# Gating logits accumulated in one bank, turned by one transposition in layer 1's banks, and one expert's weights loaded from ScalarE's queue

## Chip, core and metric

One NeuronCore of a Trainium2 chip runs the whole program as one launch. The metric is device time in microseconds (us), the median of repeated executions. TensorE does the products, VectorE, ScalarE and GpSimd the work around them, and SyncE issues most transfers. In the profile these are PE (PEld is its weight load), DVE, ACT, POOL and SP. PSUM, the memory into which TensorE writes, has eight banks of 128 partitions by 512 fp32 values.

## What is computed

A chunked attention feeds a feed-forward layer, and that feeds a mixture of experts with two experts per token:

```python
scores = scale * np.matmul(q_c, k_c.transpose(0, 1, 2, 4, 3))     # chunks of 64, 8 heads of 64
attn = softmax(scores); x = np.matmul(attn, v_c)                  # 4608 tokens of 512
h = x @ w_in; x = (h - np.tanh(h)) @ w_out                        # 512 -> 2048 -> 512
noisy_logits = x @ w_gate + np.log1p(np.exp(x @ w_noise)) * noise # 8 experts
top2 = np.argpartition(-noisy_logits, 2, axis=1)[:, :2]           # with softmax weights over the two
out[mask] += top2_w[mask, k, None] * (np.maximum(x[mask] @ w1[e], 0.0) @ w2[e])
```

## The kernel before

**Tiles and steps.** The 4608 tokens are 36 tiles of 128, in nine groups of four (g = 0 to 8). The first part of the program runs each group through the feed-forward layer in 16 steps. A step is one block of 128 of the 2048 hidden units: twelve layer-1 products (`products1`, L338; fp32 as a high and a low fp32r part, three passes over four blocks of 128) into a bank named `hp`, then `activate` (ScalarE's tanh L374, VectorE's subtraction L377 that is the last to read the bank, ScalarE's L378 and VectorE's L380 that make the two parts), and twelve layer-2 products (`products2`, L446) of the step before into four banks named `acc`. There are two `hp` banks, taken in turn by whoever asks next. The second part runs 24 groups of slots (three for each of 8 experts) in 8 steps each; there the activation is L382 on ScalarE and L385 on VectorE.

**Half-steps.** `advance` emits a step: layer 1 and its activation, the functions listed for slot h, layer 2 of the step before, the functions of slot h + 1. So an even slot stands between layer 1 and layer 2 and an odd slot behind layer 2. A group has 32 slots (`H1`), a slot group 16 (`H2`). The lists are written out by hand: `hs` for attention visits, a second `hs` for the gating of the group before, and loops for loads. Each engine runs its own instructions in the order emitted and waits for the others' semaphores.

**What stands in the slots.** An attention visit (`u_attn`) transposes the exponentials of one tile (`u_t`, L198, into an `hp` bank named `pt` that ScalarE copies out at L200), multiplies those of an older tile with v and makes the scores of a new tile (`products`, L144, in the two banks named `pair`); it then loads q, k and v of the tile two visits later on SyncE's queue. `load_v` waits until the visit's products have read the old buffer, and what is behind it on that queue waits too. The gating of group g - 1 runs within group g: `u_z` and `u_yt` load the layer's output back and transpose it in blocks of 32 on VectorE (`x2t`, L499); `u_lg` (L523) multiplies each tile's four blocks with the gate weights `wg` into the four quarters of the partitions, 512 columns in all, which ScalarE copies to `ls` (L526); `u_gate` (L542) sums the quarters and turns them with four small products against `summat`, a matrix made by `sums`. Then come short VectorE operations (`u_gate2` to `u_gate2m`), GpSimd's `u_gate3` with the running count of each expert, and `u_pos` (L640, L641), two products that give each token its place. All of these take a bank of `pair` by `misc`. Behind `u_pos` the rows are reloaded (`yr`) and scattered by GpSimd.

**Loads of experts.** `fetch_e` loads one block of an expert's two weight matrices on SyncE's queue (L282, two buffers for each of the two), and `prep_e` splits it three slots later into two parts: ScalarE L321, then VectorE or GpSimd L323. Expert 0 is loaded in group 8, expert 1 in the first two slot groups. In the second slot group `dispatched` waits until the scattered rows have landed and then issues the first loads of gathered rows (`xg`, L503) on the same queue.

The last group's gating (group 8) runs in the first slot group. The lists that set these places:

```python
hs = (1, 5, 11, 15, 20, 26) if g == 1 else (5, 14, 20, 26)              # visits
hs = (9, 11, 12, 13, 17, 18, 19, 19, 20, 23)                            # u_lg, u_gate, ..., u_gate3, u_pos
hs = (9, 12, 14, 16, 18, 19, 21, 21, 23, 24)                            # the same for g == 1
```

Of the kernel before, what the change touches and what calls it, by code (L numbers as in the profile page):

```python
# [9 lines left out]
F32 = mybir.dt.float32  # L10
# [5 lines left out]
ALU = mybir.AluOpType  # L16
# [15 lines left out]
def moe_chain_kernel(ctx: ExitStack, tc: tile.TileContext, q, k, v, w_in, w_out, wgn, noise,  # L32
                     w1, w2, out):
    nc = tc.nc
# [3 lines left out]
    NG = len(GS)  # L38
    G0 = [sum(GS[:g]) for g in range(NG)]
# [43 lines left out]
    def bank():  # L83
        return pools["pair"][:, after("pair", 2)]

    def misc(*shape):
        n = 1
        for m in shape:
            n *= m
        p = bank()[:, :n]  # L90
        return p.rearrange("p (a b) -> p a b", b=shape[1]) if len(shape) > 1 else p

    place = {G0[g] + j: (g, j) for g in range(NG) for j in range(GS[g])}
# [182 lines left out]
        nc.vector.tensor_tensor(xt[:, 1, :, c0:c0 + n], ps[:, :, :n], hi.bitcast(F32),  # L276
                                op=ALU.subtract)

    def fetch(src, tag, f=None):
        if src.dtype == F32:  # L280
            x = blk("st", "q" if tag == "wa" else "e", 2)
            nc.sync.dma_start(x, src)  # L282
            return x
        x = raws[tag][f].rearrange("p s m -> p (s m)")
        nc.sync.dma_start(x, src.bitcast(U32))
        return x
# [229 lines left out]

    def u_lg(g):
        n = GS[g]
        p = misc(n, 128)
        for j in range(n):  # L520
            x = X2T.pop(G0[g] + j)
            for d in range(4):
                nc.tensor.matmul(p[32 * d:32 * d + 32, j, :], lhsT=wg[:, d, :], rhs=x[:, d, :],  # L523
                                 start=True, stop=True, tile_position=(0, 32 * d))
        LS[g] = sp.tile([128, 4, 128], F32, name="ls", bufs=1)[:, :n]
        nc.scalar.copy(LS[g], p)  # L526

    def small(name, shape, dt=F32, bufs=1):
# [8 lines left out]

    def u_gate(g):
        n, i0 = GS[g], G0[g]
        p = misc(n, 16)  # L540
        for j in range(n):
            nc.tensor.matmul(p[:, j, :], lhsT=LS[g][:, j], rhs=summat, start=True, stop=True)  # L542
        lg = small("lg", [128, 4, 16])[:, :n, :]
        nc.scalar.copy(lg, p)
        t = small("t", [128, 4, 8])[:, :n, :]
        z = lg[:, :, 8:16]
        nc.vector.scalar_tensor_tensor(t, z, -1.0, z, op0=ALU.mult, op1=ALU.min)
        nc.scalar.activation(t, t, AF.Exp)
        GT[g] = lg, t, NZ.pop(g)
# [86 lines left out]
    def u_pos(g):  # L636
        n = GS[g]
        pay, ef, oh, mk = GT.pop(g)
        p = misc(n, 8)
        nc.tensor.matmul(p, lhsT=lower, rhs=mk[:, 0], start=True, stop=False)  # L640
        nc.tensor.matmul(p, lhsT=ones, rhs=mk[:, 1], start=False, stop=True)  # L641
        ve = nc.vector
        ps = small("ps_", [128, 4, 8])[:, :n, :]
        if g >= NG - 2:
            ve.tensor_tensor(ps, p, bump[:, None, :].to_broadcast([128, n, 8]), op=ALU.add)
        else:
            ve.tensor_copy(ps, p)
        for kk in range(2):
            ve.tensor_tensor(oh[:, :, kk, :], oh[:, :, kk, :], ps, op=ALU.mult)
        pk = small("pk", [128, 8, 1])[:, :2 * n]  # L650
        ve.reduce_sum(pk, oh.rearrange("p g k e -> p (g k) e"), axis=AX.X)
        sh = small("sh", [128, 8, 1])[:, :2 * n]
        ve.tensor_scalar(sh, pk, float(CAP), float(SHIFT), op0=ALU.is_ge, op1=ALU.mult)
        pi = small("pi", [128, 8], I32)[:, :2 * n]
        ve.tensor_tensor(pi, pk[:, :, 0], sh[:, :, 0], op=ALU.add)
        efk = ef.rearrange("p g k -> p (g k)")
        lo = small("lo_", [128, 8], I32)[:, :2 * n]
        ve.tensor_scalar(lo, pi, 127, None, op0=ALU.bitwise_and)
        hi = small("hi_", [128, 8], I32)[:, :2 * n]
        ve.tensor_scalar(hi, pi, 7, None, op0=ALU.arith_shift_right)  # L660
        fl = small("fl", [128, 8])[:, :2 * n]
        ve.scalar_tensor_tensor(fl, lo, float(NCOL), hi, op0=ALU.mult, op1=ALU.add)
        row = sp.tile([128, 2, 8], I32, name="row", bufs=2)[:, :, :2 * n]
        ve.scalar_tensor_tensor(row[:, 0], efk, float(LROWS), pi, op0=ALU.mult, op1=ALU.add)
        ve.scalar_tensor_tensor(row[:, 1], efk, float(LROWS), fl, op0=ALU.mult, op1=ALU.add)

        def scatter(to, at, src, group):
            s = nc.gpsimd.indirect_dma_start(  # L668
                out=to, out_offset=bass.IndirectOffsetOnAxis(ap=at, axis=0),
                in_=src, in_offset=None)  # L670
            tc.declare_no_dep(s.ins, group=group, reason="distinct rows")
            tc.add_to_no_dep_group(group, s.ins)
            if to is xs and g >= NG - 2:
                tc.declare_no_dep(s.ins, group="sealed", reason="bump: no rows below SEAL")
                tc.add_to_no_dep_group("late", s.ins)

        def reload(j):
            i = G0[g] + j
            y = blk("yr", "y", 4)
            nc.sync.dma_start(y, x2d[i * 128:(i + 1) * 128, :])  # L680

            def both():
                for kk in range(2):
                    c = 2 * j + kk
                    nc.gpsimd.memset(spacer, 0.0)
                    scatter(xs, row[:, 0, c:c + 1], y, "rows")
                rows_left.pop()
            loaded.append(both)

        for j in range(n):  # L690
            rows_left.append(j)
            waiting.append(L(reload, j))
        for j in range(n):
            for kk in range(2):
                c = 2 * j + kk
                waiting.append(L(scatter, lst, row[:, 1, c:c + 1], pay[:, j, kk, :], "entries"))
# [136 lines left out]
    ident = cp.tile([128, 128], F32, name="ident")  # L833
    make_identity(nc, ident)
    wg = cp.tile([128, 4, 32], F32, name="wg")
    summat = cp.tile([128, 16], F32, name="summat")
    lower = cp.tile([128, 128], BF16, name="lower")
    ones = cp.tile([128, 128], BF16, name="ones")
    nc.vector.memset(ones, 1.0)
# [8 lines left out]
    def consts():  # L848
# [12 lines left out]
        nc.vector.memset(pad, 0)  # L861
        nc.gpsimd.iota(pad[:, :, 0], pattern=[[0, NCOL // 4], [128, 4]], base=0,
                       channel_multiplier=1)

    def sums():
        nc.vector.tensor_tensor(summat, ident[:, 0:16], ident[:, 32:48], op=ALU.add)
        nc.vector.tensor_tensor(summat, summat, ident[:, 64:80], op=ALU.add)
        nc.vector.tensor_tensor(summat, summat, ident[:, 96:112], op=ALU.add)

    def store_consts():  # L870
        nc.sync.dma_start(wg[:, :, 0:16], wgn.rearrange("p (d m) -> p d m", d=4))
# [73 lines left out]
    RW = {}  # L945
# [16 lines left out]

    def fetch_e(e, f):
        if e < E:
            RW[e, f] = fetch(w1[e, f], "wa"), fetch(w2[e, f], "wb")

    def prep_e(e, f):
        if e < E:
# [83 lines left out]
    def at(h, fn, *a):  # L1052
        slots[h].append(L(fn, *a))
# [15 lines left out]
    visits = []  # L1069
    at(H1, decoded)  # L1070
    for g in range(1, NG - 1):
        hs = (1, 5, 11, 15, 20, 26) if g == 1 else (5, 14, 20, 26)
        for h in hs:
            visits.append((H1 * g + h, n0 if n0 < NT else None))
            n0 += 1
# [8 lines left out]
    for g in range(NG):  # L1084
        h0 = H1 * g
        at(h0, load_nz, g)
        if g > 0:
            n = GS[g - 1]
            for j in range(n):
                i = G0[g - 1] + j  # L1090
                at(h0 + 1 + j, u_z, i)
                at(h0 + 5 + j, u_yt, i)

            if g == NG - 1:
                hs = (9, 11, 12, 13, 15, 17, 17, 19, 20, 23)
            elif g == 1:
                hs = (9, 12, 14, 16, 18, 19, 21, 21, 23, 24)
            else:
                hs = (9, 11, 12, 13, 17, 18, 19, 19, 20, 23)
            for h, fn in zip(hs, (u_lg, u_gate, u_gate2, u_gate2h, u_gate2a, u_gate2b, u_gate2m,  # L1100
                                  u_gate2c, u_gate3, u_pos)):
                at(h0 + h, fn, g - 1)
        if g == 0:
            at(H1 + 6, sums)
            at(26, store_consts)
            for o, f in ((0, 3), (1, 2), (1, 3)):
                at(0, fetch_w, o, f)
            for f in range(NF1):
                at(2 * f, fetch_w, 0, f + 4)
                at(2 * f, prep_w, 1, f)  # L1110
                at(2 * f, decode_w, 0, f + 2)
                at(2 * f, rebias_w, 0, f + 3)
                at(2 * f + 1, fetch_w, 1, f + 4)
                at(2 * f + 1, prep_w, 0, f + 2)
                at(2 * f + 1, decode_w, 1, f + 1)
                at(2 * f + 1, rebias_w, 1, f + 2)
        else:
            for f in range(0, NF1):
                if g == 1:
                    if f < E:  # L1120
                        at(h0 + 2 * f, zero_x, 2 * f)
                        at(h0 + 2 * f, zero_x, 2 * f + 1)
                    if f == E:
                        at(h0 + 2 * f, zero_rows, xs[SEAL - 128:SEAL, :])
                elif (g - 2) * NF1 + f < NT + DUMMY // 128:
                    at(h0 + 2 * f, zero_out, (g - 2) * NF1 + f)
# [139 lines left out]
```

## Time and profile before

| what | value |
|---|---|
| time, median of 3 runs | 1734.88 us (1733.57 to 1735.49) |
| the profiled execution | 1724.89 us, of which its span is 1723.2 us |
| granted TensorE clock, mean over the span | 0.997 |
| PE busy | 1703.2 us (99%), 10386 records |
| DVE, ACT, POOL busy | 773.5, 533.4, 489.0 us |
| HBM read and written | 118.76 and 64.10 MB, 106 GB/s over the span |

The profile is one execution. Its busy times say how long an engine had work, its chain of waits what the end of the program hung on, its timeline what one engine did when, with the idle time before an instruction and what ended it. An fp32 product is two records. A row that joins several instructions (x12) starts at the first one's start, and the next row's start tells how long they held the engine; the duration in it reaches to the modelled end of the last.

### The profile page before, as it was taken

The numbers are of one execution on the slowest core, as the hardware profiler recorded it, in microseconds if no ns is written. First come the engines' busy times: TensorE is split into PE (matmuls) and PEld (weight loads), VectorE is DVE, ScalarE is ACT, GpSimd is POOL, SyncE is SP. The second block draws the span as 40 slices with busy tenths as digits, with TensorE's granted clock in tenths as the row PEclk, the third lists the DMA queues.
The fourth block names the chain that finished last, engine by engine and source line by source line (L and its number), as shares of the span: only waits on it lengthen the run. The fifth ranks groups of instructions, "written<-read, shape, count | busy, mean of one in ns | idle before, by whom it ended". The sixth has DMA issues, their size and how long they took to land.

```text
span 1723.2 us, 27349 instructions
## 1 busy us (share of the span) xinstructions
PE 1703.2 (99%) x10386; PEld 1430.1 (83%) x10389; DVE 773.5 (45%) x1912; ACT 533.4 (31%) x1036; POOL 489.0 (28%) x741
## 2 busy tenths in 40 slices
PE   8999999999999999999999999999999999999998
PEld 5788788888888888888888788988899888988887
DVE  8965545454544545443555333433333333343321
ACT  5643232322222322322332222322233222232211
POOL 4640130404040220404163622322232222222112
PEclk9999999999999999999999999999999999999999
DMA  8536253625332321312354544433354343443422
GB/s 302 206 107 159 83 163 92 194 62 173 94 112 68 114 83 56 129 32 95 98 168 117 134 113 92 102 96 80 84 111 110 74 84 89 100 99 82 73 28 38
DMA packets 198596, 185.19 MB, mean 107 GB/s; under 512 B 80928, under 2 KB 140320, under 8 KB 198432
## 3 DMA queue, kind: packets, MB, share of 16 engines
q1 hardware_dynamic: 178816, 143.00, 28.0%
q0 software_dynamic: 19328, 39.41, 11.9%
q8 instruction: 112, 1.84, 0.5%
q10 hardware_dynamic: 288, 0.52, 0.1%
q14 instruction: 52, 0.43, 0.1%
HBM read 118.76 MB, written 64.10 MB: 106 GB/s over the span
## 4 chain that ended last, share of the span: by engine, by line
PE 95%; DVE 2%; POOL 1%; issue 1%; DMA 1%; SPq 0%; ACT 0%; POOLq 0%; DVEq 0%; ACTq 0%
PE hp L338 46%; PE acc L446 45%; PE pair L144 2%; PE pt L198 1%; PE pair L523 1%; PE one L144 1%; DMA st<-in_w_dram 0%; PE pair L542 0%; SPq L503 0%; POOL xs L668 0%; PE hp L824 0%; DVE word L313 0%; DVE sm L180 0%; DVE word L307 0%; DVE x L315 0%
## 5 line engine op out<-in xcount | busy, mean ns | idle before, releaser
L338 PE MATMUL hp<-xt,wa 128*128 128x512 f32 (+5 forms) x4032 | 857.3, 362 | 0.9 <-ACT xt L214 0.9
L446 PE MATMUL acc<-wb,gt 128*128 128x512 f32 x3432 | 842.8, 392 | 3.6 <-DVE o L795 3.1
L338 PEld LDWEIGHTS hp<-xt,wa 128*128 128x128 f32 x4032 | 706.4, 189 | 111.2 <-issue 2.1
L446 PEld LDWEIGHTS acc<-wb,gt 128*128 128x128 f32 x3432 | 637.5, 188 | 135.4 <-ACT o L793 3.3
L385 DVE SCALAR_TENSOR_TENSOR gt<-hp,gt 128x384 fp32r<-128x384 f32 (+2 forms) x184 | 109.4, 594 | 428.4 <-ACT gt L382 428.2
L382 ACT ACTIVATE gt<-hp 128x384 fp32r<-128x384 f32 (+2 forms) x184 | 95.8, 521 | 434.2 <-PE hp L338 414.9
L377 DVE TENSOR_TENSOR g<-hp,g 128x512 f32<-128x512 f32 x144 | 99.5, 691 | 268.4 <-ACT g L374 268.3
L374 ACT ACTIVATE g<-hp 128x512 f32<-128x512 f32 x144 | 86.1, 598 | 355.2 <-PE hp L338 351.7
L323 POOL TENSOR_TENSOR wb<-st,wb 128x512 fp32r<-128x512 f32 x64 | 92.3, 1442 | 320.1 <-ACT wb L321 320.0
L798 POOL DMA_INDIRECT out_dram<-o,lsa x73 | 118.0, 1617 | 51.5 <-DVE o L795 29.0
L403 POOL COPY spacer<-mark 1x1 f32<-1x1 f32 x181 | 45.0, 249 | 301.4 <-DVE mark L398 224.7
L380 DVE TENSOR_TENSOR gt<-g,gt 128x512 fp32r<-128x512 f32 x128 | 89.0, 695 | 87.8 <-ACT gt L378 83.0
L378 ACT CAST gt<-g 128x512 fp32r<-128x512 f32 x144 | 89.3, 620 | 110.6 <-DVE g L377 96.5
L617 POOL TENSOR_SCALAR r<-d 128x4 f32<-128x4 f32 x9 | 2.1, 236 | 385.7 <-ACT d L608 385.7
L668 POOL DMA_INDIRECT xs<-yr,row x72 | 72.9, 1012 | 49.9 <-DMA yr<-x2d 21.7
L275 ACT CAST xt<-xg 128x512 fp32r<-128x512 f32 x80 | 48.8, 610 | 99.7 <-DVE xg L499 99.5
L276 DVE TENSOR_TENSOR xt<-xg,xt 128x512 fp32r<-128x512 f32 x80 | 54.5, 681 | 54.1 <-ACT xt L275 54.1
L668 POOL DMA_INDIRECT lst<-pay,row x72 | 71.7, 996 | 20.3 <-issue 18.4
L499 DVE STREAM_TRANSPOSE xg<-xg 128x512 f32<-128x512 f32 x80 | 56.3, 704 | 2.7 <-DMA xg<-xs 2.7
L323 DVE TENSOR_TENSOR wa<-st,wa 128x512 fp32r<-128x512 f32 x64 | 44.1, 689 | 8.6 <-ACT wa L321 8.5
L321 ACT CAST wa<-st 128x512 fp32r<-128x512 f32 x64 | 39.3, 614 | 8.4 <-DMA st<-in_w_dram 8.4
L321 ACT CAST wb<-st 128x512 fp32r<-128x512 f32 x64 | 39.7, 620 | 0.8 <-DMA st<-in_w_dram 0.7
(184 smaller groups left out, 882.7 us busy)
## 6 DMA issues: line engine op xcount, KB each, us to landing
st<-in_w_dram SPq DMA_DIRECT2D x128, 256.0 KB
xg<-xs SPq DMA_DIRECT2D x320, 64.0 KB
out_dram<-zero SPq DMA_DIRECT2D x40, 256.0 KB
x2d<-y SPq DMA_DIRECT2D x36, 256.0 KB
z<-x2d SPq DMA_DIRECT2D x144, 64.0 KB
yr<-x2d SPq DMA_DIRECT2D x36, 256.0 KB
q<-in_q_dram SPq DMA_DIRECT2D x34, 256.0 KB
vs<-in_v_dram SPq DMA_DIRECT2D x34, 256.0 KB
```

The source lines that it names most:

```text
L321: nc.scalar.copy(w[:, 0, :], x)
L323: eng.tensor_tensor(w[:, 1, :], x, w[:, 0, :].bitcast(F32), op=ALU.subtract)
L338: nc.tensor.matmul(s.hp[:, :n], lhsT=w[:, a, d, :], rhs=s.xt[:, b, d, :n], start=(i == 0), stop=(i == 11))
L374: nc.scalar.activation(g, hp[:, :n], AF.Tanh)
L377: nc.vector.tensor_tensor(g, hp[:, :n], g, op=ALU.subtract)
L378: nc.scalar.copy(hi, g)
L380: eng.tensor_tensor(lo, g, hi.bitcast(F32), op=ALU.subtract)
L382: nc.scalar.activation(hi, hp[:, :n], AF.Relu)
L385: nc.vector.scalar_tensor_tensor(lo, hp[:, :n], 0.0, hi.bitcast(F32), op0=ALU.max, op1=ALU.subtract)
L446: nc.tensor.matmul(s.grp["acc"][j][:m], lhsT=s.gt[:, a, j * 128:j * 128 + m], rhs=s.B[s.f][:, b, :], start=(s.f == 0 and i == 0), stop=(s. ...
L668: s = nc.gpsimd.indirect_dma_start(out=to, out_offset=bass.IndirectOffsetOnAxis(ap=at, axis=0), in_=src, in_offset=None)
L798: a = nc.gpsimd.indirect_dma_start(out=out, out_offset=bass.IndirectOffsetOnAxis(ap=en[:m, 0:1], axis=0), in_=o[:m], in_offset=None, compu ...
```

## The change

`u_lg` sums the four blocks of a tile in the bank: tile j has the j-th quarter of the partitions, and 128 columns in all. `u_gate` turns this with one transposition by `ident` and copies the 16 columns of each quarter. `summat` and `sums` go. In the first part (g < 8) logits, gating and positions take an `hp` bank instead of a bank of `pair`. Visits move from slots 5, 14, 20, 26 to 5, 9, 13, 24 (in group 1 from 1, 5, 11, 15, 20, 26 to 1, 5, 9, 13, 18, 24); `u_lg` stands behind the visit at 9, `u_gate` behind that at 13, `u_pos` behind that at 24. Group 8 has no visits and keeps its slots. Expert 1's sixteen loads are issued on ScalarE's queue.

```diff
-    def misc(*shape):
+    def misc(*shape, dense=False):
...
-        p = bank()[:, :n]
+        p = (pp.tile([128, 512], F32, name="hp", bufs=2) if dense else bank())[:, :n]
...
     def u_lg(g):
         n = GS[g]
-        p = misc(n, 128)
-        for j in range(n):
-            x = X2T.pop(G0[g] + j)
-            for d in range(4):
-                nc.tensor.matmul(p[32 * d:32 * d + 32, j, :], lhsT=wg[:, d, :], rhs=x[:, d, :],
-                                 start=True, stop=True, tile_position=(0, 32 * d))
-        LS[g] = sp.tile([128, 4, 128], F32, name="ls", bufs=1)[:, :n]
+        p = misc(128, dense=g < NG - 1)
+        x = [X2T.pop(G0[g] + j) for j in range(n)]
+        for d in range(4):
+            for j in range(n):
+                nc.tensor.matmul(p[32 * j:32 * j + 32], lhsT=wg[:, d, :], rhs=x[j][:, d, :],
+                                 start=(d == 0), stop=(d == 3), tile_position=(0, 32 * j))
+        LS[g] = sp.tile([128, 128], F32, name="ls", bufs=1)
         nc.scalar.copy(LS[g], p)
...
     def u_gate(g):
         n, i0 = GS[g], G0[g]
-        p = misc(n, 16)
-        for j in range(n):
-            nc.tensor.matmul(p[:, j, :], lhsT=LS[g][:, j], rhs=summat, start=True, stop=True)
+        p = misc(128, dense=g < NG - 1)
+        nc.tensor.transpose(p, LS[g], ident)
         lg = small("lg", [128, 4, 16])[:, :n, :]
-        nc.scalar.copy(lg, p)
+        nc.scalar.copy(lg, p.rearrange("p (a b) -> p a b", b=32)[:, :n, 0:16])
...
     def u_pos(g):
-        p = misc(n, 8)
+        p = misc(n, 8, dense=g < NG - 1)
...
     def fetch_e(e, f):
         if e < E:
-            RW[e, f] = fetch(w1[e, f], "wa"), fetch(w2[e, f], "wb")
+            queue = nc.scalar if e == 1 else nc.sync
+            RW[e, f] = fetch(w1[e, f], "wa", queue=queue), fetch(w2[e, f], "wb", queue=queue)
...
-        hs = (1, 5, 11, 15, 20, 26) if g == 1 else (5, 14, 20, 26)
+        hs = (1, 5, 9, 13, 18, 24) if g == 1 else (5, 9, 13, 24)
...
-                hs = (9, 12, 14, 16, 18, 19, 21, 21, 23, 24)
+                hs = (9, 13, 14, 16, 17, 19, 21, 21, 22, 24)
             else:
-                hs = (9, 11, 12, 13, 17, 18, 19, 19, 20, 23)
+                hs = (9, 13, 14, 16, 17, 18, 19, 20, 20, 24)
...
-            at(H1 + 6, sums)
```

What the change moves, at three places. First TensorE in group 2, from slot 8 to slot 12, before:

```order
L446 MATMUL acc<-wb,gt 128x512 x12
L523 MATMUL pair<-x2t,wg 32x128 x16
L338 MATMUL hp<-xt_2712,wa 128x512 x12
L446 MATMUL acc<-wb,gt 128x512 x12
L542 MATMUL pair<-summat,ls 128x16 x4
L338 MATMUL hp<-xt_2712,wa 128x512 x12
```

and, from slot 9 to slot 13, now:

```order
L198 MATMUL pt<-ident,e 128x128 x4
L144 MATMUL pair<-pts,vs 64x64 x16
L144 MATMUL pair<-ks,q 64x64 x16
L523 MATMUL hp<-x2t,wg 32x128 x16
L338 MATMUL hp<-xt_2709,wa 128x512 x12
L446 MATMUL acc<-wb,gt 128x512 x12
L338 MATMUL hp<-xt_2709,wa 128x512 x12
L446 MATMUL acc<-wb,gt 128x512 x12
L198 MATMUL pt<-ident,e 128x128 x4
L144 MATMUL pair<-pts,vs 64x64 x16
L144 MATMUL pair<-ks,q 64x64 x16
L541 MATMUL hp<-ident,ls 128x128
```

The logits stand behind the visit's products and no longer alone between two blocks of layer products, and the turning is one product instead of four.

Second, the queues in the second slot group. SyncE's queue before, from the reload of the last group's rows to its end:

```order
L680 DMA yr<-x2d 128x512 x4
L503 DMA xg<-xs 32x4x128 x12
L282 DMA st<-in_w_dram 128x512 x2
L503 DMA xg<-xs 32x4x128 x8
L471 UNCONDITIONAL_BRANCH
L282 DMA st<-in_w_dram 128x512 x2
```

and ScalarE now, from the loads of block 6 to those of block 7:

```order
L282 DMA st<-in_w_dram 128x512 x2
L382 ACTIVATE gt<-hp 128x512
L396 COPY mark<-zero 1x1
L275 CAST xt_9725<-xg 128x4x128
L321 CAST wa<-st 128x512
L321 CAST wb<-st 128x512
L382 ACTIVATE gt<-hp 128x512
L396 COPY mark<-zero 1x1
L275 CAST xt_9725<-xg 128x4x128
L282 DMA st<-in_w_dram 128x512 x2
```

The two pairs of weight loads (`st`) stood behind twelve and behind twenty loads of gathered rows; now each follows an activation of ScalarE.

Third, VectorE in the first slot group, where the last group's blocks are transposed for the logits. The names in brackets are the semaphores waited for. Before:

```order
L323 TENSOR_TENSOR wa<-st,wa 128x512 [waits DMAHW3_49,Activation_49]
L385 SCALAR_TENSOR_TENSOR gt<-hp,gt 128x384 [waits Activation_49]
L398 MEMSET mark 1x1 [waits Pool_49]
L499 STREAM_TRANSPOSE x2t<-z 128x4x4x32 [waits DMAHW2_49,DMAHW7_49,DMAHW1_49,DMAHW0_49]
L499 STREAM_TRANSPOSE x2t<-z 128x4x4x32 [waits DMAHW5_49,DMAHW6_49,DMAHW4_49,PE_49]
```

and now:

```order
L323 TENSOR_TENSOR wa<-st,wa 128x512 [waits DMAHW4_49,Activation_49]
L385 SCALAR_TENSOR_TENSOR gt<-hp,gt 128x384 [waits Activation_49]
L398 MEMSET mark 1x1 [waits Pool_49]
L499 STREAM_TRANSPOSE x2t<-z 128x4x4x32 [waits DMAHW3_49,DMAHW4_49,DMAHW2_49,DMAHW1_49]
L499 STREAM_TRANSPOSE x2t<-z 128x4x4x32 [waits DMAHW5_49,DMAHW0_49,DMAHW6_49,DMASW5_49,DMAHW7_49,DMASW4_49,DVE_49]
```

The fourth transposition waited for TensorE (its buffer was one that the logits of an earlier tile had to read first) and now waits for transfers and VectorE alone.

## Rows read from the trace of the kernel before

**Rows 1.** The page's chain that ended last, by engine

```profile
PE 95%; DVE 2%; POOL 1%; issue 1%; DMA 1%; SPq 0%; ACT 0%; POOLq 0%; DVEq 0%; ACTq 0%
```

**Rows 2.** Timeline of PE, group 2: start us, us, engine line op, names, count [idle before]

```profile
252.51 1.20 PE L523 MATMUL pair<-x2t,wg 128*32 128x128 f32 x32
253.64 3.04 PE L338 MATMUL hp<-xt,wa 128*128 128x512 f32 x12
256.52 2.88 PE L446 MATMUL acc<-wb,gt 128*128 128x512 f32 x12
259.24 0.96 PE L542 MATMUL pair<-summat,ls 128*128 128x16 f32 x8
260.05 3.03 PE L338 MATMUL hp<-xt,wa 128*128 128x512 f32 x12
262.91 2.88 PE L446 MATMUL acc<-wb,gt 128*128 128x512 f32 x12
```

**Rows 3.** Timeline of all engines, the visit at slot 5 of group 2

```profile
239.76 0.60 PE L198 MATMUL pt<-ident,e 128*128 128x128 f32 x4
...
240.29 0.69 PE L144 MATMUL pair<-pts,vs 64*64 64x64 f32 x32
240.40 0.59 ACT L200 COPY pts<-pt 128x512 f32<-128x512 f32 x1 [1.19 <-PE pt L198]
...
241.38 0.50 PE L338 MATMUL hp<-xt,wa 128*128 128x512 f32 x1
```

**Rows 4.** Timeline of PE, positions at slot 23 of group 2

```profile
296.40 0.19 PE L640 MATMUL pair<-mk,lower 128*128 128x32 bf16 x1
...
299.28 2.88 PE L446 MATMUL acc<-wb,gt 128*128 128x512 f32 x12
```

**Rows 5.** Timeline of PE, positions at slot 24 of group 1

```profile
196.05 2.88 PE L338 MATMUL hp<-xt,wa 128*128 128x512 f32 x12
...
200.86 0.18 PE L641 MATMUL pair<-mk,ones 128*128 128x32 bf16 x1 [1.56 <-POOL mk L632]
...
205.17 3.06 PE L338 MATMUL hp<-xt,wa 128*128 128x512 f32 x12
```

**Rows 6.** Windows: span, busy of PE, PEld, DVE, ACT, POOL, granted clock, DMA share, GB/s

```profile
200.00:205.00 5.00, 4.14 (x13) 3.29 (x13) 2.56 (x14) 0.62 (x1) 0.97 (x6) 0.71 0.00 0
...
982.00:989.00 7.00, 6.80 (x33) 6.20 (x34) 3.80 (x10) 2.14 (x5) 5.87 (x7) 0.76 0.63 92
```

**Rows 7.** Timeline of DVE, slot 8 of group 2, the fourth transposition

```profile
252.53 0.71 DVE L499 STREAM_TRANSPOSE x2t<-z 128x512 f32<-128x512 f32 x1
```

**Rows 8.** Timeline of PE, first slot group, the last group's logits

```profile
917.10 0.43 PE L523 MATMUL pair<-x2t,wg 128*32 128x128 f32 x8 [0.61 <-DVE x2t L499]
```

**Rows 9.** Timeline of PE, from the second slot group into the third

```profile
967.12 2.88 PE L338 MATMUL hp<-xt,wa 128*128 128x512 f32 x12
...
982.20 1.62 PE L446 MATMUL acc<-wb,gt 128*128 128x512 f32 x6 [3.14 <-DVE o L795]
...
988.00 1.59 PE L338 MATMUL hp<-xt,wa 128*128 128x256 f32 x12
989.42 1.55 PE L446 MATMUL acc<-wb,gt 128*128 128x512 f32 x6
```

**Rows 10.** Timeline of ACT, the same place: block 7 of expert 1

```profile
978.73 0.62 ACT L321 CAST wa<-st 128x512 fp32r<-128x512 f32 x1 [3.84 <-DMA st<-in_w_dram]
```

**Rows 11.** Timeline of SP, its queue at the same place

```profile
966.32 8.56 SPq L503 DMA_DIRECT2D xg<-xs  x8
974.92 0.90 SPq L282 DMA_DIRECT2D st<-in_w_dram  x2
```

**Rows 12.** Instructions of line 118: issues from ScalarE's queue, ns min/median/max

```profile
L118 ACTq DMA_DIRECT2D ks<-in_k_dram x2: 404/433/462, 0.8 to 1.3; - x2
```

**Rows 13.** Timeline of all engines, the visit at slot 26 of group 1

```profile
208.89 0.69 DVE L377 TENSOR_TENSOR g<-hp,g 128x512 f32<-128x512 f32 x1 [5.37 <-ACT g L374]
...
209.68 0.50 PE L446 MATMUL acc<-wb,gt 128*128 128x512 f32 x1
```

More of the change, by code (lines that the diff above doesn't have):

```diff
@@ L277, in split_xt, with fetch @@
                                 op=ALU.subtract)
-    def fetch(src, tag, f=None):
+    def fetch(src, tag, f=None, queue=None):
         if src.dtype == F32:
             x = blk("st", "q" if tag == "wa" else "e", 2)
-            nc.sync.dma_start(x, src)
+            (queue or nc.sync).dma_start(x, src)
             return x
@@ L835, in moe_chain_kernel @@
     wg = cp.tile([128, 4, 32], F32, name="wg")
-    summat = cp.tile([128, 16], F32, name="summat")
+    cp.tile([128, 16], F32, name="gap")
     lower = cp.tile([128, 128], BF16, name="lower")
@@ L863, in consts @@
                        channel_multiplier=1)
[L865 to L868, printed above, removed]
     def store_consts():
```

## Prediction

> **What bounds the kernel now.** I read the page's chain first: 95% of the span hangs on PE [rows 1], so what counts is time that PE spends or waits, and every other engine only where PE waits for it. Then I read PE's timeline at the places that the diff touches. A block of twelve products of 512 columns holds PE for 2.72 us (256.52 to 259.24) [rows 2]. That is the ruler: what stands between two blocks beyond it is the price of what was put there. In those rows the reader is to see that a small fp32 piece costs more than its own products, because the block behind it is longer too: 3.67 - 0.81 = 2.86 us instead of 2.72 behind the gate products. The waits came next: PE waits long at two places only, for the count of experts in group 1 [rows 5] and at the border of the second and third slot group [rows 9]. The windows show that after both the granted clock falls, to a mean of 0.71 and 0.76 of full speed, that is to 1.2 GHz for part of the window [rows 6].
>
> The sum is made against the profiled execution, 1724.89 us. The median of the runs, 1734.88 us, is 9.99 us longer; I take the difference for the same on both sides and subtract the sum from the median.
>
> **The logits, groups 1 to 7.** Alone they cost 252.51 to 256.52 less one block, 4.01 - 2.72 = 1.29 us: 1.13 for the sixteen products and 0.16 on the block behind [rows 2]. Their number and width stay; behind a visit the 0.16 is paid by the visit anyway. I take a saving of 0.16 per group, 7 x 0.16 = 1.1. Bounds: nothing, and, if sixteen products four abreast cost only what four transpositions of as many columns do (239.76 to 240.29, 0.53 [rows 3]), 0.60 more per group, 4.2 in all. I take the lower price because it is the row of these products themselves. The fourth transposed tile, which the new order needs at its fourth product, starts with the old logits at 252.53 and takes 0.71 [rows 7]; the visit put ahead of the logits lasts 1.62 us (239.76 to 241.38 [rows 3]) and covers it.
>
> **The turning, groups 1 to 7.** Four products cost 259.24 to 262.91 less one block, 3.67 - 2.72 = 0.95 us [rows 2]. One transposition behind a visit is a fifth one there, 0.53 / 4 = 0.13 [rows 3]. Saved: 0.82, 7 x 0.82 = 5.7 (lower bound 0.61, if it costs a quarter of the 0.81 and the 0.14 behind it stays).
>
> **The positions.** Alone they cost 299.28 - 296.40 - 2.72 = 0.16 us [rows 4]. Behind a visit I take half, between all and nothing: 6 x 0.08 = 0.5 for groups 2 to 7. In group 1 they cost 205.17 - 196.05 - 2 x 2.72 = 3.68 us: 1.56 us of waiting for GpSimd's count, and a layer-2 block at the lower clock behind it [rows 5, 6]. The count starts in slot 23 there, one half-step ahead of the products; the change starts it in slot 22 and puts a visit of 1.62 us ahead of the products, 2.72 + 1.62 = 4.3 us more. The wait goes, and what is late next is the activation of the block just done, which is the rival below. Saved: 3.6.
>
> Groups 1 to 7 together: 1.1 + 5.7 + 0.5 + 3.6 = 10.9 us.
>
> **Group 8** has no visits. Its turning alone costs 0.13 + 0.14 instead of 0.95: 0.68 saved. Its logits lose: the fourth tile is ready 0.73 us after their start (as at 252.53 [rows 7]), three products lie ahead of it now, thirteen behind, 13/16 of 1.13 = 0.92; they end 0.5 later than now. Net 0.2 saved.
>
> **The last group's gating, first slot group.** The order shows that the fourth transposition no longer waits for TensorE; the logits' wait of 0.61 us [rows 8] goes, and the turning saves 0.68: 1.3. Lower bound 0.7, if the tile stays late for another reason.
>
> **Expert 1's loads.** From 967.12 to 988.00 PE runs three blocks of 2.72, three layer-1 blocks of 256 columns at 1.42 (988.00 to 989.42) and two blocks of six products at 1.36, 15.1 us of work, in 20.9 us: 5.7 lost, 3.14 of it in one wait and the rest mostly at the lower clock behind it [rows 6, 9]. The wait is named for VectorE's copy of the output, but VectorE and the banks were late because ScalarE stood 3.84 us for the weights of block 7 [rows 10], with the activation and the copies queued behind. Those weights were issued at 974.92, behind loads of gathered rows that held the queue for 8.56 us [rows 11], and 3.8 us later they were there. On ScalarE's queue they are issued behind the activation of slot 12 and needed in slot 15, three half-steps or 8 us later. I take all 5.7 (bounds: 0 and 5.7). The buffer of block f was that of block f - 2, prepared five half-steps earlier, so ScalarE should not stand at the issue either; what is queued behind it there is the next evictions. Each issue holds ScalarE 0.43 us [rows 12], sixteen of them 6.9 us; they lie behind an activation, while PE runs a block of layer 2, and cost nothing. Were nothing to cover them, the sum would shrink by 6.9.
>
> The Trainium skill, "DMA: Bandwidth & Descriptors", section "Rules for kernel authors", says that spreading transfers over issuing engines does not help, since all run on the same sixteen DMA engines, and saves only issue time. By that alone this part would bring next to nothing; the trace speaks of a load that started late in a blocked queue, not of a slow one.
>
> **Costed at nothing.** The three sums of `summat` on VectorE, and a copy of 128 columns in place of 512 on ScalarE: PE waits for neither. The visits' loads are issued two visits ahead; the shortest distance, slot 5 to 13, is 8 x 2.72 = 21.8 us against the 3.8 us just seen. The reloads behind the positions move two half-steps at most, to where group 1 has them already.
>
> **Sum:** 10.9 + 0.2 + 1.3 + 5.7 = 18.1 us; 1734.9 - 18.1 = **1716.8 us**, and a span of 1705.1 us in a profile like the one shown.
>
> **Rivals.**
> (1) *The loads bring nothing*: ScalarE stands at the issue or for the weights as it did, or the border waits for something else. For it: the copies of the output are many steps behind one activation. Against: no such border waits in the other experts. 18.1 - 5.7 = 12.4: 1722.5 us.
> (2) *Layer 1's banks become the wait.* The positions in slot 24 take the bank that the block just done has filled; TensorE must wait until VectorE's L377 has read it. In the row of a visit in an even slot L377 ends at 208.89 + 0.69 = 209.58, and the visit's products end at 209.68 [rows 13]: 0.10 us to spare. In slot 13 the next block needs the copy of `pt`, done at 240.99, against 241.38 [rows 3]. If VectorE is late by as much as the 1.56 us of rows 5, each of seven groups pays what that wait cost, 3.68: 25.8 in all, 1742.6 us, slower. Short of the point where the clock falls it is at most 7 x 1.5 = 10.5: 1727.3. Against: VectorE was idle for 5.37 us before that L377 [rows 13].
> (3) *The logits do not fit behind a visit*: going from the visit's 64-wide pieces to quarters costs as much again as the 0.16 that going back to whole blocks costs. The saving on the logits turns into a loss of the same size: 7 x 0.32 = 2.2 less, 1719.0 us. Against: the block behind the gate products, which use the whole array, is as much longer (0.14) as that behind the logits in quarters (0.16) [rows 2], and the visit's own step from whole array to 64-wide pieces shows no gap (240.29 is 239.76 and four transpositions [rows 3]). The Trainium skill, "TensorEngine Tiling (Array Packing)", section "Key Properties", has it as a rule that a change of tiling mode drains TensorE, which would speak for this rival.
>
> **Chances.** As summed 0.64; rival 1 0.14; rival 3 0.09; rival 2 short waits 0.05, about as before 0.05, slower 0.03. A measurement of this kernel tells about 0.2%, 3.5 us, from no change. The first four are faster (0.92); same 0.05; slower 0.03. The range runs from the sum with the cheaper logits (1716.8 - 4.2 = 1712.6) and a measurement's spread of 1.6 below it to rival 1 with the lower bounds of turning and logits (1722.5 + 1.5 + 1.1) and as much above: 1711 to 1726.
>
> **What would show it.** In the profile after: records of the turning fall from 72 to 18 and those of the logits stay 288; the row of L640 or L641 waiting for POOL in group 1 is gone; the wait on L795 at the second border and ScalarE's wait for `st` are gone, with no window at a lower clock in either place; expert 1's `st` appear on ACTq. Wrong would be: new waits of L338 or the positions for L377 or L200 in groups 1 to 7 (rival 2), a wait of the same size at the border (rival 1), or logits that hold PE longer than 1.13 us behind a visit (rival 3).

## The result and the profile after

| what | before | after |
|---|---|---|
| time, median of 5 runs each | 1735.29 us (1733.57 to 1735.71) | 1705.97 us (1705.78 to 1707.25) |
| ratio | | 0.9836 [0.9824, 0.9849] |
| the profiled execution | 1724.89 us, span 1723.2 | 1707.0 us, span 1705.2 |

The change saved 29.3 us; 18.1 were forecast, and 1716.8 us with a range from 1711 to 1726. Yet the forecast span was 1705.1 us and the profile of after has 1705.2: against the profile that it was made on, the sum comes out within 0.1 us, part of which is luck (see the sum below). After's profiled execution agrees with its other runs, before's was 10 us shorter than its others. So the question for the runs was what before loses in those executions and after does not.

The chain of after, by engine, beside [rows 1]:

```profile
PE 97%; DVE 1%; ACT 1%; issue 0%; another core or an unknown queue 0%; POOL 0%; POOLq 0%; DVEq 0%; ACTq 0%
```

PE's timeline of after, group 2 (start us, us, engine line op, names, count), first the logits, then the turning, then the positions, each behind a visit, beside [rows 2, 4]:

```profile
250.80 1.08 PE L523 MATMUL hp<-x2t,wg 128*32 128x128 f32 x32
251.81 3.01 PE L338 MATMUL hp<-xt,wa 128*128 128x512 f32 x12
254.66 2.88 PE L446 MATMUL acc<-wb,gt 128*128 128x512 f32 x12
...
264.45 0.33 PE L541 MATMUL hp<-ident,ls 128*128 128x128 f32 x1
264.54 3.02 PE L338 MATMUL hp<-xt,wa 128*128 128x512 f32 x12
267.39 2.88 PE L446 MATMUL acc<-wb,gt 128*128 128x512 f32 x12
...
296.22 0.19 PE L639 MATMUL hp<-mk,lower 128*128 128x32 bf16 x1
...
296.28 3.02 PE L446 MATMUL acc<-wb,gt 128*128 128x512 f32 x12
```

The turning now holds PE 0.09 us and the positions 0.06, and the block behind each is 2.85 or 2.86 us, against 2.88 behind a visit alone (306.34 to 309.22 in the profile of before). In group 1 the positions no longer wait [rows 5], and the border of the second and third slot group has no gap [rows 9]:

```profile
200.16 0.19 PE L639 MATMUL hp<-mk,lower 128*128 128x32 bf16 x1
...
200.22 3.02 PE L446 MATMUL acc<-wb,gt 128*128 128x512 f32 x12
...
963.60 1.59 PE L338 MATMUL hp<-xt,wa 128*128 128x256 f32 x12
965.04 1.55 PE L446 MATMUL acc<-wb,gt 128*128 128x512 f32 x6
```

### The profile page after: what moved, and what is told of

The parts are those of the page before. It is cut to its first block, busy times and chain, and to the rows that moved or that the text cites. A ratio compares the mean times of both kernels' runs of the same rounds, so it can differ in the third digit from the quotient of the medians.

```text
span 1705.2 us, 27189 instructions
## 1 busy us (share of the span) xinstructions
PE 1690.2 (99%) x10325; PEld 1422.1 (83%) x10326; DVE 773.8 (45%) x1909; ACT 529.6 (31%) x1036; POOL 493.5 (29%) x741
## 4 chain that ended last, share of the span: by engine, by line
PE 97%; DVE 1%; ACT 1%; issue 0%; another core or an unknown queue 0%; POOL 0%; POOLq 0%; DVEq 0%; ACTq 0%
PE hp L338 47%; PE acc L446 46%; PE pair L144 2%; PE pt L198 1%; PE one L144 1%; PE hp L523 0%; PE hp L823 0%; POOL out_dram L797 0%; DVE sm L180 0%; DVE e L164 0%; DVE word L313 0%; DVE g L377 0%; PE hp L541 0%; DVE mx L157 0%
## 5 line engine op out<-in xcount | busy, mean ns | idle before, releaser
L219 DVE TENSOR_TENSOR xt<-pair,xt 128x512 fp32r<-128x512 f32 x32 | 22.1, 689 | 41.1 <-ACT xt L214 41.1
```

## Experiments

**Before once more, for a second and a third profile (no edit).**

> The kernel before, unchanged, for a second profile. The prediction subtracted its sum (18.1 us) from the median of 1735 us and took the 10 us by which the one profiled execution (1724.9 us) was shorter for the same on both sides; the changed kernel took 1706, as if they belonged to the kernel before alone. If such executions differ in one place, a second profile of about 1733 us span shows there 10 us more than the first: theory 1 says at the border of the second and third slot group (980 to 990 us), theory 2 in group 1 behind the wait for the count (200 to 210 us), theory 3 spread over groups 1 to 7. If the 10 us belong to timing and not to the program, its span is again about 1723 us while its times are 1735.

> The kernel before, unchanged, a third profile. In one set of executions it took 1734.0 us and stood 10 times, 3.9 us, for nothing that the profile shows within the scores of the visits of slot 26; in the next set it took 1726.0 us. If the two levels differ by that stall alone: at a time near 1734 us the ten rows are there, at a time near 1725 none of them is.

The second run took 1734.67 us (before beside it 1734.02) with a span of 1731.9, the third 1725.68 (before beside it 1724.9) with 1724.4. Executions of before thus come at two levels, one per set of runs made together: medians of 1734 to 1738 us (upper) and of 1725 to 1726 us (lower). The profile that the prediction was made on is of the lower, all timed runs of before in the tables are of the upper. PE's waits in the upper profile (engine, tile, line, what it waited for: us in all, times, longest), and its timeline at the visit of slot 26 in group 2:

```profile
PE pair L144 <- issue: 3.9, 10, 0.5
```

```profile
306.09 0.60 PE L198 MATMUL pt<-ident,e 128*128 128x128 f32 x4
...
307.13 0.73 PE L144 MATMUL pair<-ks,q 64*64 64x64 f32 x12
308.26 0.36 PE L144 MATMUL pair<-ks,q 64*64 64x64 f32 x6 [0.40 <-issue]
309.01 0.49 PE L144 MATMUL pair<-ks,q 64*64 64x64 f32 x14 [0.38 <-issue]
309.42 3.02 PE L446 MATMUL acc<-wb,gt 128*128 128x512 f32 x12
```

The same visit in the third profile, at the lower level:

```profile
306.54 0.60 PE L198 MATMUL pt<-ident,e 128*128 128x128 f32 x4
...
308.19 3.03 PE L446 MATMUL acc<-wb,gt 128*128 128x512 f32 x12
```

"Issue" is time in which PE waits for nothing that the profile shows. The visit takes 309.42 - 306.09 = 3.33 us in one and 1.65 in the other. Groups 2 to 6 have two such rows each, and their visits of slot 26 take 3.33, 3.03, 3.02, 3.03 and 3.05 us, 15.5 in all, against 8.3 in the first profile: 7.2 us of the 8.7 by which the span is longer (1731.9 - 1723.2). The other 1.45 us lie ahead of the first block of group 0, which starts at 20.77 here and at 19.32 in the first profile; in after it starts at 20.52, so the first profile, and not before as such, was short by that part. First the profile of before, then after:

```profile
19.32 3.85 PE L338 MATMUL hp<-xt,wa 128*128 128x512 f32 x15 [0.91 <-ACT xt L214]
```

```profile
20.52 2.79 PE L338 MATMUL hp<-xt,wa 128*128 128x512 f32 x11 [0.91 <-ACT xt L214]
```

The next runs ask what makes the longer visits and which part of the change removes them.

**Only the loads.** Expert 1's loads on ScalarE's queue in before, and back on SyncE's in after:

```diff
...
-            RW[e, f] = fetch(w1[e, f], "wa"), fetch(w2[e, f], "wb")
+            queue = nc.scalar if e == 1 else nc.sync
+            RW[e, f] = fetch(w1[e, f], "wa", queue=queue), fetch(w2[e, f], "wb", queue=queue)
```

> Before, with expert 1's sixteen loads on ScalarE's queue and nothing else. The part was predicted at 5.7 us. Theory 1 (the 10 us that only most executions of the kernel before have belong to this border, where a load is late): 1735.3 - 5.7 - 10.1 = about 1719.5 us. Theories 2 and 3 (group 1's stall, or the gating products): 1735.3 - 5.7 = about 1729.6. The loads bring nothing: 1735.

> The change, with expert 1's loads back on SyncE's queue. Theory 1 (the 10 us sit at the border): 1706.0 + 5.7 + 10.1 = about 1721.8 us. Theories 2 and 3: 1706.0 + 5.7 = about 1711.7 us. If both parts of the change are needed to lose them, neither this kernel nor before with the loads alone shows more than 5.7.

Before with the loads moved: 1727.64 us, 6.4 less than 1734.02; the idle rows of slot 26 stay (11, 4.5 us). After with the loads moved back: 1711.86, 5.9 more than 1705.97, with the wait at the border back. From its waits:

```profile
PE acc L446 <- DVE o L794: 2.5, 1, 2.5
```

Both agree with 5.7; theory 1 (the missing 10 us sit at this border) is out.

**Only group 1.** In before, the count half a step earlier (`u_gate3` from slot 23 to 22); then all of group 1's new slots, still in the banks of `pair`:

```diff
-                hs = (9, 12, 14, 16, 18, 19, 21, 21, 23, 24)
+                hs = (9, 12, 14, 16, 18, 19, 21, 21, 22, 24)
```

```diff
-        hs = (1, 5, 11, 15, 20, 26) if g == 1 else (5, 14, 20, 26)
+        hs = (1, 5, 9, 13, 18, 24) if g == 1 else (5, 14, 20, 26)
-                hs = (9, 12, 14, 16, 18, 19, 21, 21, 23, 24)
+                hs = (9, 13, 14, 16, 17, 19, 21, 21, 22, 24)
```

> Before, with the count of group 1 (u_gate3) started in slot 22 in place of 23, so that the positions do not wait for GpSimd, and nothing else. The stall was predicted at 3.6 us. Theory 2 (the 10 us belong to this stall and the lower clock behind it): 1735.3 - 3.6 - 10.1 = about 1721.6 us. Theories 1 and 3: 1735.3 - 3.6 = about 1731.7 us.

> Before, with group 1's visits and gating in the slots of the change (visits 1, 5, 9, 13, 18, 24; count in 22; positions behind the visit of 24), in the banks of pair and with the old logits. The prediction has 3.6 us for group 1's stall, from the count one half-step earlier and the visit ahead of the positions; the count one half-step earlier alone brought nothing, as VectorE's part of it stood behind the division of the visit of slot 20. With that visit in slot 18 and one ahead of the positions: 1734.0 - 3.6 = about 1730.4. If the lower clock behind the stall was not the stall's doing: 1734.0 - 1.8 = 1732.2.

The first took 1734.8 us beside 1734.02: nothing, and PE waits for the count as before. The count's VectorE part (L624) stands behind the division of the visit of slot 20 on VectorE, in whichever of the two slots it is listed. VectorE's timeline, first this kernel, then after (where the cast is L623):

```profile
198.36 0.69 DVE L188 TENSOR_TENSOR e<-e,sm 128x512 f32<-128x512 f32 x1
...
199.06 0.14 DVE L624 CAST ef<-i 128x8 f32<-128x8 uint32 x1
```

```profile
195.36 0.69 DVE L380 TENSOR_TENSOR gt<-g,gt 128x512 fp32r<-128x512 f32 x1 [0.69 <-ACT gt L378]
...
196.07 0.14 DVE L623 CAST ef<-i 128x8 f32<-128x8 uint32 x1
```

With that visit in slot 18 the cast no longer has the division ahead of it. After needs the visit ahead of the positions as well: there GpSimd's last mask (L631) is done at 198.80, behind the end of the block at 198.54 and ahead of the positions at 200.16. All the new slots without the new banks took 1737.36 us beside 1726.02: 11.3 us slower, where 3.6 were to be saved. Its PE waits:

```profile
PE pair L640 <- DVE e L164: 3.6, 1, 3.6
PE pair L523 <- DVE e L164: 2.8, 1, 2.8
PE pair L542 <- DVE e L164: 2.8, 1, 2.8
```

The gating asks for a bank of `pair` that still holds the scores of the visit just done, until VectorE's L164 has read them.

**After, with the old banks.** The edit takes `dense=g < NG - 1` out of the three calls of `misc`.

> The change, with the logits, the turning and the positions of groups 1 to 7 in the two banks of pair as before. In group 1 of before the new slots without the new banks cost three waits of 2.8 to 3.6 us for VectorE's subtraction, the last to read the visit's scores, and 1737.4 - (1726.0 - 3.6) = 15.0 us in all with the lower clock behind them. If the banks of layer 1 are what lets these products stand behind a visit: 7 x 9.2 to 7 x 15.0 us more, 1706.0 + 64 to 105 = 1770 to 1811 us. If only the slots matter: 1706.

1800.09 us, 94 more than after. Three of its PE waits:

```profile
PE pair L639 <- DVE e L164: 21.3, 6, 3.6
PE pair L523 <- DVE e L164: 19.3, 7, 2.8
PE pair L541 <- DVE e L164: 16.5, 6, 2.8
```

57.1 us of waits, and 4.2 for L219; the granted clock falls to a mean of 0.982 (0.998 in after). Slots and banks are one change: the banks of layer 1 are what lets the products stand behind a visit.

**Only the sums in the bank and the one transposition**, in the banks of `pair` and the old slots (the change's `u_lg` and `u_gate` without `dense`).

> Before, with the logits summed in the bank and one transposition, in the banks of pair and in the old slots. The turning alone: 0.95 becomes 0.27 in nine places, 6.1 us; the logits, alone in their slot, wait for the fourth transposed tile, up to 0.5 us in eight groups. Theory A (the stall of slot 26 stays): between 1734.0 - 6.1 = 1727.9 and 1731.9. If fewer small instructions were what ends the stall: 8.6 less, 1719.3 to 1723.3.

1720.48 us beside 1726.02: 5.5 less, at the lower level, so that it says nothing on the stall. PE's timeline, group 2, from the second part of the logits on:

```profile
252.32 1.06 PE L523 MATMUL pair<-x2t,wg 128*32 128x128 f32 x26 [0.36 <-DVE x2t L499]
...
258.87 0.27 PE L541 MATMUL pair<-ident,ls 128*128 128x128 f32 x1
258.90 3.00 PE L338 MATMUL hp<-xt,wa 128*128 128x512 f32 x12
261.73 0.62 PE L446 MATMUL acc<-wb,gt 128*128 128x512 f32 x2
```

Alone, the turning costs 261.73 - 258.87 - 2.72 = 0.14 us (0.95 before, [rows 2]), and the logits lose to the late fourth tile, as was forecast for group 8.

**The place of the last visit.** In before from slot 26 to 24, ahead of the scatters, in three sets; in after from 24 to 27, in two:

```diff
-        hs = (1, 5, 11, 15, 20, 26) if g == 1 else (5, 14, 20, 26)
+        hs = (1, 5, 11, 15, 20, 26) if g == 1 else (5, 14, 20, 24)
```

> Before, with the last visit of groups 2 to 7 in slot 24 in place of 26, and nothing else. In the second profile of before TensorE stands twice with nothing that the profile shows (10 times, 3.9 us) within the score products of that visit in groups 2 to 6; each such visit takes 3.33 us from its first transposition to the next block, 1.61 in the first profile. Theory A: TensorE runs out of instructions because that visit falls among the scatters of gathered rows, which start 5.2 us behind the positions of slot 23; in slot 24 the visit is over before they start. Then 5 x 1.72 = 8.6 us go: 1734.0 - 8.6 = about 1725.4. Theory B: the visit outruns its instructions wherever it stands (so many small products in a row, the fourth visit of a group): no change, 1734.

> Before, with the last visit of groups 2 to 7 in slot 24, a second time. Where before takes near 1734 us, theory A expects 8.6 us less, about 1725, theory B no change; where before takes about 1725, both expect no change, as was measured (1723.6 against 1726.0).

> Before, with the last visit of groups 2 to 7 in slot 24, a third time. Where before takes near 1734 us: theory A (scatters starve TensorE) 8.6 us less, about 1725, with no idle rows in the scores; theory B (the visit outruns its instructions) no change. Where before takes about 1725: 1723.5, as measured.

> The change, with the last visit of groups 2 to 7 in slot 27, as far behind the positions (slot 24) as slot 26 is behind slot 23 in before. Theory A (visits among the scatters starve): 1706.0 + 8.6 + 0.5 (positions no longer behind a visit) = about 1715.1 us, with idle time before the score products in groups 2 to 6 ended by nothing that the profile shows. Theory B, or that the shorter list of instructions cured it: about 1706.5.

> The change, with the last visit of groups 2 to 7 in slot 27, a second time. Where before takes near 1734 us, theory A expects 1706.0 + 8.6 + 0.5 = about 1715.1 us with idle rows in the scores of groups 2 to 6; theory B, or that the shorter list of instructions cured it, about 1706.5. Where before takes about 1725: 1706.4, as measured.

The first two sets were at the lower level (before 1726.02 and 1724.9): slot 24 took 1723.64 and 1723.49, and after with slot 27 took 1706.37 and 1706.38. So slot 27 told nothing of the theories, and 1706 us beside either level (at the lower one with slot 27 only) says that the change, with its visits there, has no such two levels. The third set was at the upper level: before 1738.09, slot 24 1730.18, 7.9 less, with no idle row in any score. The place alone removes the stall; theory B, by which the visit outruns its instructions wherever it stands, is out. But 1730.18 is still 6.5 us above 1723.64, and the profile is of the fastest of those five runs (1726.56 us, the others 1730.14 to 1731.85), so what the others lose stays open.

**Deeper among the scatters.** The same entry set to 29, in before and in after, in that third set:

> Before, with the last visit of groups 2 to 7 in slot 29 in place of 26: deeper among the scatters, where the share of the DMA engines is over 1.0 for some 6 us (0.4 to 0.5 at slot 26). Theory A: idle rows in its scores wherever before has them, as many or more (1734 or above), and perhaps where before has none. Theory B, and that the stall belongs to one instant of slot 26: about 1725 us.

> The change, with the last visit of groups 2 to 7 in slot 29, among the scatters that follow the positions of slot 24. Theory A: where before stands (near 1734 us), 1706.0 + 8.6 + 0.5 = about 1715 us with idle rows in the scores of groups 2 to 6; where it does not, about 1706.5. That the change cured the stall by its shorter list of instructions: about 1706.5 in both.

Before took 1762.01 us (23.9 more), after 1718.13 (12.1 more than 1705.97). PE's timeline of the first, group 2, and of the second, group 3:

```profile
312.35 0.60 PE L198 MATMUL pt<-ident,e 128*128 128x128 f32 x4
...
314.09 0.36 PE L144 MATMUL pair<-ks,q 64*64 64x64 f32 x5 [0.37 <-issue]
314.85 0.34 PE L144 MATMUL pair<-ks,q 64*64 64x64 f32 x4 [0.40 <-issue]
315.57 0.35 PE L144 MATMUL pair<-ks,q 64*64 64x64 f32 x5 [0.39 <-issue]
317.02 0.48 PE L144 MATMUL pair<-ks,q 64*64 64x64 f32 x4 [1.10 <-issue]
```

```profile
406.90 0.36 PE L144 MATMUL pair<-ks,q 64*64 64x64 f32 x4 [0.21 <-issue]
```

Before has 22 such rows (14.3 us) and a wait of 3.0 us for a bank of `pair` besides, after 13 (4.4 us). After is open to the same stall; its shorter list of instructions does not cure it, the place of its visits does.

**Which transfers.** Before with slot 29, once with the reloads and scatters of groups 2 and 3 begun only in group 4 (with a third buffer for `pay` and `row`, which they read), once without the stores of zeros (the output is then not cleared):

```diff
...
+        if 1 <= g <= 2:
+            LATER.append(begin)
+        else:
+            begin()
...
+            if g == 4:
+                at(h0 + 1, u_begin)
```

```diff
-                elif (g - 2) * NF1 + f < NT + DUMMY // 128:
+                elif 16 <= (g - 2) * NF1 + f < 0:
```

> Before with the last visit in slot 29, and with the reloads and scatters that belong to groups 2 and 3 held back until group 4 begins; the rest of the traffic stays. Read by the rows of the profile, not by the time, since held-back scatters cost elsewhere. Theory A (reloads and scatters starve TensorE): no idle rows in the scores of the visits of groups 2 and 3 (before with the visit in slot 29: 5 and 4 rows, 3.2 and 2.9 us), idle rows in groups 4 to 6 as there (4 or 5 each). If other traffic (zero stores, the visits' own loads) does it: idle rows in all five groups.

> Before with the last visit in slot 29, and without the stores of zeros to the output in groups 2 to 8, which share SyncE's queue and the DMA engines with the reloads; the output is not cleared. Theory A (reloads and scatters alone): idle rows in the scores of groups 2 to 6 as with the stores (22 rows, 14.3 us). If the stores of zeros do it: none. If the sum of the traffic counts: fewer and shorter.

With the scatters held back (1770.41 us, before beside it 1736.03; 11.5 us of it is one wait ahead of group 4's logits, so the rows tell and not the time) the late visits of groups 2 and 3 have no idle row. In group 4, where the held-back scatters run, the visit of slot 20 has six and that of slot 5 one; no other kernel here has one in these slots. PE's timeline, the late visit of group 2 and the visit of slot 20 of group 4:

```profile
314.59 0.60 PE L198 MATMUL pt<-ident,e 128*128 128x128 f32 x4
...
316.21 3.04 PE L338 MATMUL hp<-xt,wa 128*128 128x512 f32 x12
```

```profile
502.18 0.37 PE L144 MATMUL pair<-ks,q 64*64 64x64 f32 x5 [0.40 <-issue]
```

Without the stores of zeros (1758.35 us) there are 24 rows, 13.5 us. The stall needs the reloads and scatters of gathered rows; the zeros have no part.

The scatters alone are not enough. In group 3 GpSimd issues them at the same instants of the visit at either level. The third profile, where that visit takes 1.65 us (next block at 404.88):

```profile
403.08 0.96 POOL L668 DMA_INDIRECT xs<-yr,row  x1 [0.64 <-issue]
403.23 0.60 PE L198 MATMUL pt<-ident,e 128*128 128x128 f32 x4
```

The second profile, where it takes 3.03 us (next block at 407.48):

```profile
404.31 0.97 POOL L668 DMA_INDIRECT xs<-yr,row  x1 [0.64 <-issue]
404.45 0.60 PE L198 MATMUL pt<-ident,e 128*128 128x128 f32 x4
```

The next scatter follows 1.12 us behind the visit's start in one (404.35) and 1.13 in the other (405.58).

**The scatters later, the visits where they were.** Before with reloads and scatters of groups 2 to 7 held back to slot 27.

> Before, with the reloads and scatters of groups 2 to 7 held back until slot 27, so that the visit of slot 26 is over before the first scatter; the visits stay. Only where before stands in slot 26 (near 1734 us) does it tell the theories apart. Theory A (the scatters starve TensorE of instructions): 8.6 us less, about 1725.4. Theory B (the visit outruns its instructions without them): no change. Where before takes about 1725 us both expect no change.

A miss: at the lower level, where there was no stall to remove, it took 1736.88 us beside 1724.9, since the reloads share their buffers with layer 2's output. Its PE waits:

```profile
PE acc L446 <- DVE y L491: 8.5, 5, 4.1
```

## Why the prediction was right, and where it was wrong

**The step that failed** is the one between the sum and the median: "The median of the runs, 1734.88 us, is 9.99 us longer; I take the difference for the same on both sides and subtract the sum from the median." By before's second profile some 7.2 of the 9.99 us were a stall of before alone, in a visit that the change happens to move ahead of the scatters. Another 1.2 to 1.8 were the first profile's early start (its first block stands at 19.32, that of after at 20.52, those of before's other two profiles at 20.77 and 21.14); the rest is within what executions of one level differ by. The shown runs (1733.57 to 1735.49) against 1724.89 said that the profile lacked something that all of them had; a rival in which the change removes it too would have stood at 1716.8 - 10.0 = 1706.8, and the range should have reached there. Of the 11.2 us saved beyond the forecast, then, 7.2 are the stall and 1.2 the early start; the other 2.8 are how the medians stand to single profiled executions (1735.29 to 1733.65 of before's second profile, 1705.97 to 1707.0 of after's).

**The sum.** The logits of group 8 start at 817.85 in after and at 829.58 in the profile of before, 11.7 us earlier; with the 1.2 us by which after starts later (20.52 against 19.32) groups 1 to 7 saved 12.9, 10.9 forecast. Those of the first slot group start at 904.11 against 915.62: group 8 lost 0.2 where 0.2 was to be gained. The rest, 18.0 - 11.5 = 6.5 us, is the last group's gating and the loads, 7.0 forecast. That the total agrees with the two spans to 0.1 us is luck: the 2.0 us too little in groups 1 to 7 stand against the late start and the 0.9 too much behind. Measured from the first block on, the sum is 1.1 us too small. First before, then after:

```profile
829.58 1.20 PE L523 MATMUL pair<-x2t,wg 128*32 128x128 f32 x32
...
915.62 0.86 PE L523 MATMUL pair<-x2t,wg 128*32 128x128 f32 x24
```

```profile
817.85 0.42 PE L523 MATMUL hp<-x2t,wg 128*32 128x128 f32 x6
818.63 1.06 PE L523 MATMUL hp<-x2t,wg 128*32 128x128 f32 x26 [0.36 <-DVE x2t L499]
...
904.11 1.08 PE L523 MATMUL pair<-x2t,wg 128*32 128x128 f32 x32
```

**The logits** hold PE 1.01 us behind a visit, where alone they cost 1.29: 0.28 saved in place of 0.16, and rival 3 is out (it asked for more than 1.13). Alone they also made the block ahead of them longer (249.70 to 252.51, 2.81 us in place of 2.72), which the prediction left out. **The turning** saves 0.86 (0.95 - 0.09), 0.82 forecast; its records are 9, not 18, since a transposition is one record here. **The positions** save 0.10, 0.08 forecast. With the 0.02 to 0.03 less on each block behind, a group such as group 4 saves 1.4 us in place of 1.06.

**Group 1's stall** went, and for part of the reason given. The step "the count starts in slot 23 there [...]; the change starts it in slot 22" is worth nothing by itself; what moved the count was the visit of slot 20, whose division was ahead of it on VectorE. The visit put ahead of the positions was named in the prediction and does its part; no run takes the two one by one.

**The banks** were costed at nothing. Rival 2 looked for a danger in those of layer 1, where none of its waits came; that without them the new slots cost 94 us was not seen, because the prediction never asked what the same products would wait for in `pair`.

**The loads** were right: 5.7 forecast, 6.4 and 5.9 measured, and rival 1 is out. The Trainium skill, "DMA: Bandwidth & Descriptors", section "Rules for kernel authors", has it that spreading transfers over issuing engines gains only issue time; these runs show a gain from starting late loads earlier, which that rule does not cover: of the 8.56 us that the queue was held [rows 11], SyncE stood 4.9 waiting for VectorE to have read a buffer of `xg`, and the weights behind it on the queue waited too.

## What to carry to other kernels

Before adding a sum to a median, ask what the runs have that the profile lacks: if they differ by more than their own spread, the change may move just that, and the forecast needs a case for it. On this evidence a burst of many small products is safer where GpSimd issues no scatters; look for idle rows ended by "issue". When small work is put behind other work, ask first which buffer it takes and who still reads it.

## What was not expected of the hardware

TensorE stood still while it waited for nothing that the profile shows. In the stalled visits it does mostly four to six records of 64 columns at a time, one lot in 0.73 us or so (314.09, 314.85, 315.57), and the weight loads wait alike. In the worst stretch it is not for want of transfer capacity. The windows of before with the visit in slot 29 (span, busy of PE, PEld, DVE, ACT, POOL, granted clock, DMA share, GB/s):

```profile
312.00:315.00 3.00, 2.24 (x57) 1.72 (x56) 0.52 (x2) 0.59 (x1) 2.46 (x5) 1.00 0.43 175
315.00:318.00 3.00, 1.02 (x13) 0.83 (x12) 0.00 (x0) 0.00 (x0) 2.12 (x3) 0.84 0.04 6
```

In the worst three microseconds the DMA engines move 6 GB/s, and what goes on is GpSimd's issue of scatters of `lst`, eight bytes per row:

```profile
315.14 0.98 POOL L668 DMA_INDIRECT lst<-pay,row  x1 [0.16 <-issue]
```

The nearest reading is that TensorE's instructions come late while GpSimd issues scatters; no run shows it directly. The Trainium skill, "Runtime: NRT & Kernel Launch", section "Instruction fetch mechanics", describes instructions as streamed in by transfers of their own and that cost as mostly hidden. The profile lists those transfers as queues of their own, and from 519 to 524 us, around the stall of group 4, none of them moves anything, only the scatters' queue does; if instructions come late there, it is not for such a transfer. Two things stay open: whether GpSimd's issuing or the writes themselves do it (both were held back together, and with them the reloads, of whose transfers nothing moves there either), and what sets the level, which the scatters alone do not, since before was at the upper one in four of the six sets, that of the result among them, and at the lower in two and in the first profile.
